# Splitting one weight piece over two DMA queues, and reading the residual from rows that are already loaded

## The chip, the cores and the metric

The kernel runs on 1 core of one Trainium2 chip. The metric is the device time of one execution in microseconds (us). Before the change its median is 773.24 us over 3 runs (773.04 to 773.42).

## What is computed

One decode step for a batch of B = 2 tokens with model width D = 1024. A layer norm of x feeds two branches, and both are added to x itself, the residual:

```python
xn = _layernorm(x)                                  # x is (2, 1, 1024), no scale or shift
q  = (xn @ wq).reshape(2, 1, 32, 128)               # 32 query heads, 4 key and value heads
p  = softmax(q @ k_cache^T * 128 ** -0.5)           # k_cache, v_cache: (2, 4, 32768, 128)
A  = (p @ v_cache).reshape(2, 1, 4096) @ wo
Bo = silu(xn @ w1) @ w2                             # w1: 1024 x 3584, w2: 3584 x 1024
return x + A + Bo
```

All of it is float32. With two tokens the work is reading: the two caches (268 MB) and the weights pass through the core once.

## The kernel before

**Two buffers and one queue.** `bufA` and `bufB` hold 128 partitions x 16384 floats (8 MB each). SyncE (SP) issues all large loads on its own DMA queue, q1 in the profile, alternately into the two buffers, in a fixed order: `wq[0]`, `wq[1]`, `w1b`, `w1a`, then for each of the 8 pairs of a head and a token two loads of keys and two of values, then `wo[0]`, `wo[1]`, `w2a` (two halves) and last `w2b`. Before each load SP waits (`freed`) until TensorE is through with what the buffer held; `load()` (L161 to L164) does this. A load is spread over 16 DMA engines, and each of these works through its share of q1 in order.

**The end of the stream.** `w2b` is the last load, 12 x 1024 floats in each of 128 rows. It comes in seven pieces, cut by `cuts`: 6 D, 2 D, D, D, D, then 4 * CUT = 768 floats and the last 256 floats of each row. Each has its own semaphore (`ld[1]`, `more[1]`, `last[0]` to `last[4]`), so TensorE can begin on a piece when it lands. The five pieces of `last` are used by `tile(0)` to `tile(4)`, each 8 float32 matmuls into the PSUM tile `acc`. Their order on TensorE is written out by hand at the end of the function: tile 0, tile 1, then two products that fold the sum of everything else (`ob`) into `acc`, then tiles 2, 3 and 4. ScalarE copies `acc` to `ot` (L242), and SP writes `ot` to memory (L330) and waits for it.

**The sum of everything else.** ScalarE copies the partial products of `wo` and `w2` from PSUM to `ev[0]`, `ev[1]`, `ev[2]` (L240), each as soon as TensorE has finished them. GpSimd (POOL) copies the lhs weights for the next load into `weights` (L317), adds `ev[1]` to `ev[0]` (L319), adds the residual `xres` (L321) and `ev[2]` (L323); VectorE adds the two halves (L325) and then the first part of `w2b` (L327), which gives `ob`.

**x at the start.** ScalarE's DMA queue (q10) brings x in two small transfers. `x8` (L115) is 8 rows of 1024 floats into every 16th partition of `xs`: the two tokens four times, each copy rotated by another quarter, because only the first 256 columns of `xs` are normalised and transposed; the four copies cover the four quarters in different partitions. `x` (L117) is 4 rows of 512 floats into every 16th of the first 64 partitions of `xres`, a slice of the zeroed tile `blank`, for the residual.

Of the kernel before, what the change touches and what calls it, by code (L numbers as in the profile page):

```python
# [8 lines left out]
B, HQ, HKV, SK, DH, D, F = 2, 32, 4, 32768, 128, 1024, 3584  # L9
P = 128  # L10
REP = HQ // HKV
W = 16384
NC = SK // W
KT = D // P
FT = F // P
QW = D // 4
CUT = 3 * QW // 4
LOOPS = HKV * B
STEPS = 4 + 4 * LOOPS + 4
# [29 lines left out]
        self.eng.sem_inc(token, -n)  # L49


def gqa_plus_mlp_kernel(nc, x, x8, kt, v0, v1, wq, wo, w1a, w1b, w2a, w2b, out):


    pe, dve, act, pool = (Stream(nc, e, n) for e, n in
                          ((nc.tensor, "pe"), (nc.vector, "dve"), (nc.scalar, "act"), (nc.gpsimd, "pool")))
    sp, T, V, A, G = nc.sync, nc.tensor, nc.vector, nc.scalar, nc.gpsimd
    sems = [pe.sem, dve.sem, act.sem, pool.sem]

    def sem(name):  # L60
        sems.append(nc.alloc_semaphore(name))
        return sems[-1]

    def sb(name, *shape):
        return nc.alloc_sbuf_tensor(name, shape, F32).ap()
# [3 lines left out]

    buf = [sb(n, P, W) for n in ("bufA", "bufB")]  # L70
    ld, more, tok = ([sem(f"{n}{k}") for k in "AB"] for n in ("ld", "more", "tok"))
    ldx, ldr, done, turn_sem, self_sem = (sem(n) for n in ("ldx", "ldr", "done", "marks", "self"))
    freed, subbed, normed, tq, pself = (sem(n) for n in ("freed", "subbed", "normed", "tq", "pself"))
    trm, tgd, tls, tob = (sem(n) for n in ("trm", "tgd", "tls", "tob"))
    last = [sem(f"last{i}") for i in range(5)]
# [3 lines left out]
    xs, xT = sb("xs", P, D), sb("xT", P, KT, 32)  # L79
    stats, mv, ln = sb("stats", P, 2, V.BN_STATS_DIM), sb("mv", P, 2), sb("ln", P, 6)  # L80
    ev = [sb(f"ev{i}", P, 1024) for i in range(4)]
# [2 lines left out]
    pre, sig, rsig = sb("pre", P, FT, 32), sb("sig", P, FT, B), sb("rsig", P, FT, B)  # L84
    onew = sb("onew", P, REP)
    ones = sb("ones", P, P)
    blank, used = sb("blank", P, P + 32 + 160 + 3 * REP + 1024 + 32 * (HQ + FT)), [0]

    def zeroed(*shape):
        n = shape[0] * (shape[1] if len(shape) > 1 else 1)  # L90
        lo = used[0]
        used[0] += n
        t = blank[:, lo:lo + n]
        return t.rearrange("p (a m) -> p a m", m=shape[1]) if len(shape) > 1 else t

    ident, sel, fold, rm, lsum, gd, ob, xres = (zeroed(n) for n in (P, 32, 160, REP, REP, REP, 512, 512))
    oT, hT = zeroed(HQ, 32), zeroed(FT, 32)
    rest, ot = sb("rest", P, 512), sb("ot", P, QW)
    gm, gmax, rl = sb("gm", REP, 1), sb("gmax", P, 1, REP), sb("rl", P, REP)
# [5 lines left out]
    def mm(o, lhsT, rhs, start=True, stop=True):  # L105
# [7 lines left out]
    z = pool.mark(G.memset(blank, 0.0))  # L113
    act.wait(z_x)
    A.dma_start(xs[::16, :], x8).then_inc(ldx, 16)  # L115
    act.wait(z)
    A.dma_start(xres[0:64:16, :], x).then_inc(ldr, 16)  # L117
    sp.wait_ge(ldx, 16)
    sp.dma_start(buf[1], wq[1]).then_inc(ld[1], 16)

# [1 line left out]
    t = pool.mark(G.affine_select(out=ident, in_=ident, compare_op=ALU.not_equal, fill=1.0, base=0,  # L122
                                  pattern=[[-1, P]], channel_multiplier=1))
    pool.wait(t)
    halves = fold[:, 32:].rearrange("p (a m) -> p a m", m=64)[:, :, :32]
    t = pool.mark(G.tensor_add(halves, *(ident[:, 64 * g:64 * g + 64].rearrange("p (a m) -> p a m", m=32)
                                         for g in range(2))))
# [6 lines left out]
    for i in range(2):  # L134
        t = dve.mark(V.bn_stats(stats[:, i, :], xs[:, i * 512:(i + 1) * 512]))
    dve.wait(t)
    t = dve.mark(V.bn_aggr(mv, stats))
    var, std, y0, t0, t1, rstd = (ln[:, i:i + 1] for i in range(6))
    dve.wait(t)
    t = dve.mark(V.tensor_scalar_add(var, mv[:, 1:2], EPS))  # L140
    act.wait(t)
    t = act.mark(A.activation(std, var, AF.Sqrt))
    for f in (lambda: V.reciprocal(y0, std), lambda: V.tensor_mul(t0, y0, y0), lambda: V.tensor_mul(t1, t0, var),
# [5 lines left out]
        t = dve.mark(f())  # L149
# [11 lines left out]
    def load(k, dst, src, s, n):  # L161
        if n:
            sp.wait_ge(freed, n)
        sp.dma_start(buf[k][:, dst] if isinstance(dst, slice) else dst, src).then_inc(s, 16)  # L164
# [10 lines left out]
    load(0, slice(0, W // 2), w2a[:, :W // 2], ld[0], STEPS - 3)  # L175
    load(0, slice(W // 2, W), w2a[:, W // 2:], more[0], 0)
    cuts = [0, 6 * D, 8 * D, 9 * D, 10 * D, 11 * D, 11 * D + 4 * CUT, 12 * D]
    for lo, hi, s in zip(cuts, cuts[1:], [ld[1], more[1], *last]):
        load(1, slice(lo, hi), w2b[:, lo:hi], s, STEPS - 2 if lo == 0 else 0)


    for n in range(4):
        act.wait((freed, n + 1))
        t = act.mark(A.copy(ev[n], ps[n % 2]))
# [4 lines left out]
        a, b = ev[n][:, :512], ev[n][:, 512:]  # L189
        if n < 2:  # L190
            i_sumq = pool.mark(G.tensor_add(sumq[:, 512 * n:512 * n + 512], a, b))  # L191
        elif n == 2:
            t = pool.mark(G.tensor_add(sumh[:96, 512:], a[:96, :384], b[:96, :384]))
            for j in range(3):
                pool.wait(t)
                t = pool.mark(G.tensor_add(sumh[96:, 512 + P * j:512 + P * (j + 1)], a[32 * j:32 * j + 32, 384:],
                                           b[32 * j:32 * j + 32, 384:]))
# [15 lines left out]
    t = dve.mark(V.transpose(pre.rearrange("p t m -> p (t m)"), sumh))  # L213

    act.wait(t)
    t = act.mark(A.activation(sig, pre[:, :, ::16], AF.Exp, scale=-1.0))
    for f in (lambda: V.tensor_scalar_add(sig, sig, 1.0), lambda: V.reciprocal(rsig, sig),
              lambda: V.tensor_mul(hT[:, :, ::16], pre[:, :, ::16], rsig)):
        dve.wait(t)
        t = dve.mark(f())  # L220
# [16 lines left out]
    outs = []  # L237
    for n in range(3):
        act.wait((freed, STEPS - 3 + n))
        outs.append(act.mark(A.copy(ev[n], ps[n % 2])))  # L240
    act.wait((pe, 2))
    i_ot = act.mark(A.copy(ot, acc))  # L242
# [74 lines left out]
        G.tensor_copy(wt[c][:, :2 * n].rearrange("p (t d) m -> p t d m", d=2),  # L317
                      hT[:, 16 * c:16 * c + n, None, :].to_broadcast([P, n, 2, 32])).then_inc(tok[c], 1)
    t = pool.mark(G.tensor_add(ev[0], ev[0], ev[1]))  # L319
    pool.wait(t, (ldr, 16))  # L320
    t = pool.mark(G.tensor_add(ev[0][:, :512], ev[0][:, :512], xres))  # L321
    pool.wait(t, outs[2])
    t = pool.mark(G.tensor_add(ev[0], ev[0], ev[2]))  # L323
    dve.wait(t)
    t = dve.mark(V.tensor_add(rest, ev[0][:, :512], ev[0][:, 512:]))  # L325
# [64 lines left out]
    def quarter(o, lhsT, w, start=False, stop=False):  # L390
        return [mm(o[32 * j:32 * j + 32, :], lhsT[j], w[j], start, stop) for j in range(4)][-1]

    def tile(t, o, lo, n, start=False, stop=False):
        T.wait_ge(last[t], 16)
        at = buf[1][:, lo:lo + 4 * n].rearrange("p (j n) -> p j n", j=4)
        return quarter(o, [hT[:, min(24 + t, FT - 1), :]] * 4, [at[:, j] for j in range(4)], start, stop)

    pe.mark(tile(0, acc, 8 * D, QW, True))
    tile(1, acc, 9 * D, QW)
    T.wait_ge(tob, 1)  # L400
    for c in range(2):
        mm(acc, fold[:, 32 - 32 * c:160 - 32 * c], ob[:, c * QW:(c + 1) * QW], False, False)
    tile(2, acc, 10 * D, QW)
    tile(3, acc[:, :CUT], 11 * D, CUT)
    pe.mark(tile(4, acc[:, CUT:], 11 * D + 4 * CUT, QW - CUT, False, True))
# [46 lines left out]
```

## Time and profile before

| what | value |
|---|---|
| median of 3 runs | 773.24 us (773.04 to 773.42) |
| the profiled execution: its own time | 773.19 us |
| its span, first to last instruction | 771.8 us |
| around the span | 1.39 us |
| TensorE busy | 396.3 us (51%) |
| VectorE, GpSimd, ScalarE busy | 132.4, 45.4, 28.4 us |
| bytes moved by DMA | 331.43 MB, mean 429 GB/s |

The profile is of one execution, so sums are made against 773.19 us. Engines: PE is TensorE, PEld its weight loads, DVE VectorE, ACT ScalarE, POOL GpSimd, SP SyncE; a q behind the name (SPq, ACTq) is the engine's sequencer, which issues DMAs. L106 is the helper that issues every matmul, L44 the helper that passes a semaphore on, so those lines stand for many places. In a table by windows the columns are the window, its length, the busy time of each engine with the number of instructions, the granted TensorE clock, the mean busy share of the 16 DMA engines and GB/s. Packets are counted where they start, so the share in a short window can be over 1.

### The profile page before, as it was taken

Reading aid. Unit: us, or ns where it says so; the run is one execution under the profiler, and the core shown is the slowest. Engines: PE = TensorE matmul, PEld = TensorE weight load, DVE = VectorE, ACT = ScalarE, POOL = GpSimd, SP = SyncE. Lnnn points to the kernel's source line nnn. Section 1 sums busy time; section 2 is a strip of 40 time slices with the busy share of each in tenths; the row PEclk is TensorE's granted clock in tenths of the full one; section 3 lists DMA queues with packets and bytes.
Section 4 is the critical chain, followed back from the end, with each engine's and each line's share of the span. In section 5 each row is a group of like instructions: output and inputs, shape, how many; then the busy total and the mean of one; then the engine's idle time right before and its main releaser. Section 6 shows DMA issues by size and latency. Waiting matters only on the chain. (4 is left out here: it accounts for less than half of the span.)

```text
span 771.8 us, 6114 instructions
## 1 busy us (share of the span) xinstructions
PE 396.3 (51%) x2702; PEld 126.3 (16%) x2702; DVE 132.4 (17%) x99; ACT 28.4 (4%) x37; POOL 45.4 (6%) x73
## 2 busy tenths in 40 slices
PE   0545545464546454545454546554545454545566
PEld 0111111121112111211121112111211121112122
DVE  2000103030403030303130403031303130303000
ACT  0000100100010001000100010001000100010000
POOL 3001200001000100010001000100010001000121
PEclk9976766767776667776767776667776777776688
DMA  9999999999999999999999999999999999999997
GB/s 383 435 435 435 435 435 435 435 435 435 435 435 435 435 435 435 435 431 435 435 435 435 435 435 435 435 435 435 428 435 435 431 435 421 425 431 425 431 433 329
DMA packets 6953, 331.43 MB, mean 429 GB/s; under 512 B 780, under 2 KB 924, under 8 KB 1448
## 3 DMA queue, kind: packets, MB, share of 16 engines
q1 hardware_dynamic: 6928, 331.37, 99.4%
q10 hardware_dynamic: 24, 0.04, 0.0%
q8 instruction: 1, 0.02, 0.0%
HBM read 331.39 MB, written 0.02 MB: 429 GB/s over the span
## 5 line engine op out<-in xcount | busy, mean ns | idle before, releaser
L106 PE MATMUL xy<-bufB,weights 128*32 128x512 f32 x1248 | 179.6, 740 | 167.4 <-PEq L49 167.4
L106 PE MATMUL xy<-bufA,weights 128*32 128x512 f32 x1280 | 183.7, 738 | 96.9 <-PEq L49 96.9
L106 PEld LDWEIGHTS xy<-bufB,weights 128*32 128x32 f32 x1248 | 49.4, 133 | 297.8 <-issue 297.7
L106 PEld LDWEIGHTS xy<-bufA,weights 128*32 128x32 f32 x1280 | 50.6, 132 | 213.5 <-issue 213.4
L257 DVE STREAM_TRANSPOSE st<-xy 128x2048 f32<-128x2048 f32 x8 | 18.5, 2317 | 243.2 <-PE xy L106 243.2
L270 DVE TENSOR_REDUCE blank<-xy 128x512 f32<-128x2048 f32 x8 | 18.3, 2292 | 224.5 <-PE xy L106 224.5
L285 POOL MEMSET weights<- 128x1024 f32 x16 | 15.2, 951 | 525.4 <-POOLq L49 525.4
L106 PE MATMUL smA<-blank 128*8 128x128 f32 x20 | 5.4, 371 | 51.9 <-PEq L49 51.9
L106 PE MATMUL smA<-blank,ones 128*128 128x8 f32 x18 | 4.9, 347 | 50.6 <-PEq L49 50.6
L259 DVE TENSOR_REDUCE blank<-st 128x8 f32<-128x2048 f32 x8 | 30.5, 3808 | 0.3
L271 DVE TENSOR_REDUCE blank<-weights 128x8 f32<-128x2048 f32 x8 | 30.4, 3799 | 0.0
L233 ACT ACTIVATE weights<-st 128x1024 f32<-128x1024 f32 x16 | 16.0, 1048 | 328.3 <-DVE st L267 328.3
L267 DVE TENSOR_TENSOR st<-st,gmax 128x2048 f32<-128x2048 f32 x8 | 18.3, 2291 | 0.3
L106 PE MATMUL smB<-blank 128*128 128x8 f32 x72 | 15.9, 350 | 0.0
L106 PEld LDWEIGHTS smB<-blank 128*128 128x128 f32 x72 | 15.6, 318 | 0.0
L106 PEld LDWEIGHTS smA<-blank,ones 128*128 128x128 f32 x18 | 4.3, 298 | 58.5 <-issue 58.5
L236 ACT COPY blank<-onew 128x8 f32<-128x8 f32 x8 | 1.6, 204 | 279.5 <-DVE onew L275 279.5
L106 PEld LDWEIGHTS smA<-blank 128*8 128x8 f32 x20 | 1.3, 88 | 60.2 <-issue 60.2
L325 DVE TENSOR_TENSOR rest<-ev 128x512 f32<-128x512 f32 x1 | 0.7, 691 | 49.2 <-POOL ev L323 49.2
L290 POOL COPY weights<-qall 128x128 f32 x32 | 8.4, 291 | 4.2 <-POOL weights L285 3.1
L106 PE MATMUL smB<-blank,ones 8*128 8x8 f32 x20 | 5.3, 334 | 5.7 <-PEq L49 5.7
L209 DVE STREAM_TRANSPOSE tqs<-sumq 128x1024 f32<-128x1024 f32 x1 | 1.2, 1246 | 39.2 <-POOL sumq L191 39.2
(53 smaller groups left out, 58.2 us busy)
## 6 DMA issues: line engine op xcount, KB each, us to landing
bufA<-in_w2a SPq DMA_DIRECT2D x2, 4096.0 KB, 22.5
bufA<-in_w1b SPq DMA_DIRECT2D x1, 6144.0 KB, 23.7
bufB<-in_w2b SPq DMA_DIRECT2D x1, 3072.0 KB, 17.1
bufB<-in_w2b SPq DMA_DIRECT2D x3, 512.0 KB, 20.8
bufB<-in_w2b SPq DMA_DIRECT2D x1, 1024.0 KB, 19.2
bufB<-in_w2b SPq DMA_DIRECT2D x1, 384.0 KB, 22.1
bufA<-in_kt SPq DMA_DIRECT2D x8, 27.4
bufB<-in_kt SPq DMA_DIRECT2D x8, 29.0
```

Of the source, the lines that this page charges most:

```text
L106: return T.matmul(o, lhsT, rhs, start=start, stop=stop)
L209: i_q = dve.mark(V.transpose(tqs.rearrange("p c m -> p (c m)"), sumq))
L233: A.activation(wt[c].rearrange("p e m -> p (e m)"), st[:, 1024 * c:1024 * c + 1024], AF.Exp, scale=SCALE).then_inc(tok[c], 1)
L236: A.copy(oT[:, REP * h:REP * (h + 1), 16 * b], onew).then_inc(tq, 1)
L257: t = mine(V.transpose(st, xy))
L259: V.tensor_reduce(rm, e8.rearrange("p n m -> p m n"), AX.X, ALU.max).then_inc(trm, 1)
L267: V.tensor_sub(e8, e8, gmax.to_broadcast([P, 256, REP])).then_inc(subbed, 1)
L270: V.tensor_reduce(ob, xy.rearrange("p (c n) -> p n c", c=4), AX.X, ALU.add).then_inc(tob, 1)
L271: V.tensor_reduce(lsum, weights.rearrange("p e (r m) -> p m (e r)", m=REP), AX.X, ALU.add).then_inc(tls, 1)
L285: G.memset(wt[c], 0.0).then_inc(pself, 1)
L290: m = G.tensor_copy(o, q[:, None, None, :].to_broadcast([P, 4, 4, REP]))
L325: t = dve.mark(V.tensor_add(rest, ev[0][:, :512], ev[0][:, 512:]))
```

## The change

The piece of `w2b` that `tile(3)` uses (768 floats of each row) is no longer one transfer of 128 rows on SP's queue. SP brings its rows 0 to 63. ScalarE's queue brings rows 64 to 113 (50 rows) and rows 114 to 127 (14 rows), issued between the second wait for `freed` and the second of the three copies at L240; this is the wait that SP's first `w2b` load has too. `tile(3)` waits for three transfers (48) in place of one (16).

The transfer of `x`, its semaphore `ldr`, the slice `xres` and the two waits that belong to them are gone. The residual is added from `xs[:64, 256:768]`, which holds x as it was loaded. For this the copies in `x8` have their quarters in another order, and on the host the rows of `wq` and `w1` are put in the order that goes with it. `blank`, which is zeroed at the start, has 512 columns fewer.

```diff
-def gqa_plus_mlp_kernel(nc, x, x8, kt, v0, v1, wq, wo, w1a, w1b, w2a, w2b, out):
+def gqa_plus_mlp_kernel(nc, x8, kt, v0, v1, wq, wo, w1a, w1b, w2a, w2b, out):
...
-    blank, used = sb("blank", P, P + 32 + 160 + 3 * REP + 1024 + 32 * (HQ + FT)), [0]
+    blank, used = sb("blank", P, P + 32 + 160 + 3 * REP + 512 + 32 * (HQ + FT)), [0]
...
     A.dma_start(xs[::16, :], x8).then_inc(ldx, 16)
-    act.wait(z)
-    A.dma_start(xres[0:64:16, :], x).then_inc(ldr, 16)
...
-    for lo, hi, s in zip(cuts, cuts[1:], [ld[1], more[1], *last]):
-        load(1, slice(lo, hi), w2b[:, lo:hi], s, STEPS - 2 if lo == 0 else 0)
+    def part(i, rows):
+        return (buf[1][rows, cuts[i]:cuts[i + 1]], w2b[rows, cuts[i]:cuts[i + 1]])
+
+    for i, s in enumerate([ld[1], more[1], *last]):
+        load(1, *part(i, slice(0, 64 if i == 5 else P)), s, 0 if i else STEPS - 2)
...
         act.wait((freed, STEPS - 3 + n))
+        if n == 1:
+            for lo, hi in ((64, 114), (114, P)):
+                A.dma_start(*part(5, slice(lo, hi))).then_inc(last[3], 16)
         outs.append(act.mark(A.copy(ev[n], ps[n % 2])))
...
-    pool.wait(t, (ldr, 16))
-    t = pool.mark(G.tensor_add(ev[0][:, :512], ev[0][:, :512], xres))
+    pool.wait(t)
+    t = pool.mark(G.tensor_add(ev[0][:64, :512], ev[0][:64, :512], xs[:64, 256:768]))
...
-        T.wait_ge(last[t], 16)
+        T.wait_ge(last[t], 48 if t == 3 else 16)
...
-    w1 = np.asarray(B_w1)
+    wq, w1 = (np.asarray(a).reshape(4, QW, -1)[[2, 0, 1, 3]].reshape(D, -1) for a in (A_wq, B_w1))
...
-        "x": np.ascontiguousarray(xr.reshape(B, 2, 512).transpose(1, 0, 2)).reshape(4, 512),
-        "x8": np.stack([np.roll(xr, -QW * g, axis=1) for g in range(4)]).reshape(8, D),
+        "x8": np.stack([xr.reshape(B, 4, QW)[:, o] for o in ((2, 0, 1, 3), (0, 2, 3, 1), (1, 0, 2, 3), (3, 0, 1, 2))]
+                       ).reshape(8, D),
```

More of the change, by code (lines that the diff above doesn't have):

```diff
@@ L71, in gqa_plus_mlp_kernel @@
     ld, more, tok = ([sem(f"{n}{k}") for k in "AB"] for n in ("ld", "more", "tok"))
-    ldx, ldr, done, turn_sem, self_sem = (sem(n) for n in ("ldx", "ldr", "done", "marks", "self"))
+    ldx, done, turn_sem, self_sem = (sem(n) for n in ("ldx", "done", "marks", "self"))
     freed, subbed, normed, tq, pself = (sem(n) for n in ("freed", "subbed", "normed", "tq", "pself"))
@@ L94, in zeroed @@
         return t.rearrange("p (a m) -> p a m", m=shape[1]) if len(shape) > 1 else t
-    ident, sel, fold, rm, lsum, gd, ob, xres = (zeroed(n) for n in (P, 32, 160, REP, REP, REP, 512, 512))
+    ident, sel, fold, rm, lsum, gd, ob = (zeroed(n) for n in (P, 32, 160, REP, REP, REP, 512))
     oT, hT = zeroed(HQ, 32), zeroed(FT, 32)
@@ L434 @@
         "v1": lay(v[:, :, 1], (B, HKV, 2, 4, 4, 4, 4, 32, DH), (0, 1, 4, 7, 2, 5, 6, 3, 8), (B, HKV, P, W)),
-        "wq": np.stack([lay(A_wq, qd, (4, 0, 3, 1, 6, 2, 5, 7), (2, P, W))[0],
-                        lay(A_wq, qd, (4, 0, 3, 1, 2, 6, 5, 7), (2, P, W))[1]]),
+        "wq": np.stack([lay(wq, qd, (4, 0, 3, 1, 6, 2, 5, 7), (2, P, W))[0],
+                        lay(wq, qd, (4, 0, 3, 1, 2, 6, 5, 7), (2, P, W))[1]]),
         "wo": np.stack([lay(A_wo, split, (0, 4, 1, 3, 5, 2, 6), (2, P, W))[0],
```

## The prediction

> **What bounds the kernel now.** The page comes first, for the load on the DMA queues, together with the table by windows for the middle of the run and the waits of SP's queue.
>
> ```profile
> span 771.8 us, 6114 instructions
> ...
> q1 hardware_dynamic: 6928, 331.37, 99.4%
> q10 hardware_dynamic: 24, 0.04, 0.0%
> q8 instruction: 1, 0.02, 0.0%
> ```
>
> ```profile
> 40.00:740.00 700.00, 364.53 (x2458) 116.68 (x2462) 127.01 (x85) 23.46 (x31) 31.03 (x57) 0.73 1.00 433
> ```
>
> ```profile
> SPq L164 <- DVEq L44: 719.8, 38, 22.7
> ```
>
> SP's queue, q1, fills the 16 DMA engines for 99.4% of their span. From 40 to 740 us they are busy all the time (share 1.00) at 433 GB/s, that is 433 / 16 = 27.1 GB/s for one engine, while TensorE has 364.53 of 700 us. SP waits 719.8 us for a buffer and still the engines do not run dry, because the load before is then in flight. So time is bytes over 433 GB/s, plus a start and a tail, and only the bytes and the tail can be changed by this edit. The tail is next: the chain of waits, then the timeline of the last microseconds.
>
> ```profile
> 745.78 20.84 DMA bufB<-in_w2b
> 766.62 0.04 issue
> 766.66 2.91 PE acc L106 x36
> 769.57 0.02 issue
> 769.59 0.37 ACT ot L242
> ```
>
> ```profile
> 761.85 3.64 PE L106 MATMUL xy<-bufB,weights 128*32 128x512 f32 x32 [1.07 <-PEq L49]
> ...
> 766.16 0.69 DVE L327 TENSOR_TENSOR blank<-rest,xy 128x512 f32<-128x512 f32 x1 [1.00 <-PE acc L106]
> 766.66 0.64 PE L106 MATMUL acc<-bufB,blank 128*32 128x256 f32 x8 [0.64 <-DMA bufB<-in_w2b]
> 767.23 1.13 PE L106 MATMUL acc<-blank 128*128 128x256 f32 x4
> 768.29 1.23 PE L106 MATMUL acc<-bufB,blank 128*32 128x256 f32 x24
> 768.88 0.48 PEld L106 LDWEIGHTS acc<-bufB,blank 128*32 128x32 f32 x16 [0.43 <-DMA bufB<-in_w2b]
> ```
>
> The chain goes back from the output to a landing at 766.62. That is not the last piece: 36 matmuls follow it, 8 of tile 1, 4 of the fold and 24 of tiles 2, 3 and 4, so it is the landing of tile 1's piece. From there TensorE runs nearly without a gap to 769.57. The weight loads at 768.88 are the one place where it still waits for data: tile 3, the piece that the change splits. Tile 2 begins at 768.29, and 8 matmuls of that size took 767.23 - 766.66 = 0.57 us of TensorE's time at tile 1, so tile 3 could have begun at about 768.86 or a little earlier, and began at 768.88. The split piece thus holds the end by some hundredths of a microsecond, at most 0.1; the landing of tile 1 sets the rest.
>
> The windows show how the queue runs out.
>
> ```profile
> 764.00:766.00 2.00, 2.00 (x24) 0.47 (x16) 0.69 (x1) 0.00 (x0) 0.43 (x1) 1.00 1.01 403
> 768.00:768.15 0.15, 0.15 (x2) 0.00 (x0) 0.00 (x0) 0.00 (x0) 0.00 (x0) 1.00 0.16 55
> 768.15:768.36 0.21, 0.21 (x5) 0.07 (x8) 0.00 (x0) 0.00 (x0) 0.00 (x0) 1.00 0.04 15
> 768.36:768.72 0.36, 0.36 (x9) 0.09 (x8) 0.00 (x0) 0.00 (x0) 0.00 (x0) 1.00 0.07 23
> 768.72:769.20 0.48, 0.48 (x12) 0.17 (x11) 0.00 (x0) 0.00 (x0) 0.00 (x0) 1.00 0.00 0
> ```
>
> From 768.15 to 768.72 the share is 0.04 to 0.07, and one engine of 16 is 0.0625. So one engine works alone for the last 768.72 - 768.15 = 0.57 us. I take it that it is late by that much at every piece, tile 1's too. The q8 row names a candidate for the cause: one packet of 0.02 MB, about 0.6 to 0.7 us of one engine at 27.1 GB/s.
>
> **The split piece.** These are the transfers, from the list of DMA issues.
>
> ```profile
> bufB<-in_w2b SPq DMA_DIRECT2D x1, 384.0 KB, 22.1
> ...
> blank<-in_x ACTq DMA_DIRECT2D x1, 8.0 KB
> ```
>
> A row of the piece is 384 KB / 128 = 3 KB. At 403 GB/s, the rate at the tail, one engine moves 25.2 GB/s, so a row costs it 3072 / 25.2 = 0.122 us. Half the piece, 192 KB, is 0.49 us of all 16 engines.
>
> The change keeps the bytes. It takes 0.49 us of work from q1 at its end and puts the same work on q10 from about 745 us on, where ScalarE's wait for `freed` ends:
>
> ```profile
> 744.47 1.01 ACT L240 COPY ev<-xy 128x1024 f32<-128x1024 f32 x1 [16.70 <-DVEq L44]
> ...
> 745.54 0.61 POOL L317 COPY weights<-blank 128x512 f32<-128x512 f32 x1 [16.60 <-ACT ev L240]
> ...
> 748.57 1.26 POOL L321 TENSOR_TENSOR ev<-ev,blank 128x512 f32<-128x512 f32 x1
> 762.06 2.38 POOL L323 TENSOR_TENSOR ev<-ev 128x1024 f32<-128x1024 f32 x1 [12.23 <-ACT ev L240]
> ```
>
> The engines are full at that time, so whatever q10 moves early pushes q1 back. Everything between, tile 1's piece included, lands later; only tiles 3 and 4 get it back. If the 64 rows weigh equally on all engines, the landing of tile 1 goes from 766.62 to 767.11 and the 2.91 us of TensorE follow it. Tile 3 and tile 4 land as before, and so the hundredths up to 0.1 that tile 3 cost are gained back. The end moves by 0.49 less 0.02 to 0.1: about +0.43.
>
> No row shows which engines 50 or 14 rows go to, so the bounds come from the late engine. If it gets none of the 64 rows, tile 1's data on it stays at 766.62, and the others are 0.57 us ahead. Should ten of these get six rows each, they lose 6 x 0.122 = 0.73 and land at 766.62 - 0.57 + 0.73 = 766.78, so +0.16 at most and -0.1 at best. If the late engine is one that gets six rows, it is +0.73. The even split lies between, and I take that value, because nothing here tells which engine is late.
>
> [...]
>
> **ScalarE's two issues.** They stand ahead of the second copy at L240, and behind that copy wait POOL's L317, L319 and L321, then TensorE's last load of 128x512 products.
>
> ```profile
> 1.72 1.15 ACTq L115 DMA_DIRECT2D xs<-in_x  x1
> 4.49 0.53 ACTq L117 DMA_DIRECT2D blank<-in_x  x1
> ```
>
> Two issues cost 2 x 0.53 to 2 x 1.15, so 1.1 to 2.3 us. POOL's L317 would end at 746.15 + 2.3 = 748.5 at the latest, and TensorE needs it at 761.85. L321 would end at 749.83 + 2.3 = 752.1, and POOL's next step, L323, starts at 762.06 after ScalarE's third copy. So it costs nothing, with 10 to 13 us of cover. Without the cover the whole 1.1 to 2.3 us would show.
>
> **x at the start, and the residual.** The transfer that is gone is 8 KB: 8192 / 433 = 0.02 us of all engines. Its issue took 0.53 us of ScalarE while the first weights were loading.
>
> ```profile
> 1.62 2.84 POOL L113 MEMSET blank<- 128x3288 f32 x1
> ...
> 10.78 1.29 DVE L135 BATCH_NORM_STATS2 stats<-xs 128x6 f32<-128x512 f32 x2 [10.78 <-DMA xs<-in_x]
> ```
>
> The memset of `blank` loses 512 of 3288 columns, 0.44 us of POOL; but VectorE starts the norm at 10.78, when `xs` has landed, long after POOL is done, so this is hidden. The order of quarters changes no instruction. L321 works on 64 partitions in place of 128, with the same 512 columns: I keep its 1.26 us, and in either direction it has the cover above. `ldr` ended long before L321, so its wait goes for nothing. Together -0.02 us.
>
> Sum: 773.19 + 0.43 - 0.02 = 773.6 us for an execution like the profiled one. The median of the runs, 773.24, is 0.05 above it, which I do not add; it is within their spread.
>
> **The rivals.** *The late engine is spared.* Then tiles 3 and 4 come early and tile 1 on time: -0.1 at best, about 773.1. For it speaks the engine alone at the end; against it, that tile 1 and not the last piece sets the end, so the 0.57 us cannot be cashed in. Chance 0.22.
>
> *Both halves collide inside.* Rows 0 to 63 alone are written by all engines, and rows 64 to 127 beside q1's. If partitions in one half are written at half speed, each 192 KB costs 0.98 in place of 0.49 us: tile 1 is late by 0.98 and tile 3 by 0.49, so the end is about +0.9: 774.1. Nothing before writes only half of the partitions with such a load, so the profile speaks neither way. [...] Chance 0.25.
>
> *Few engines carry the 50 rows: slower.* The place is q10's first transfer. With it on 2 engines, each has 25 rows, 25 x 0.122 = 3.05 us, and tile 1 waits for them: 773.19 + 3.05 - 0.1 = 776.1. It decides from (1.55 + 0.1) / 0.122 = 14 rows on the late engine, or 1.65 + 0.57 = 2.22 us, 18 rows, on another. In the first 20 us the q10 transfers of 8 and 4 rows left 12 small packets,
>
> ```profile
> DMA packets 150, 8.25 MB, mean 412 GB/s; under 512 B 12, under 2 KB 12, under 8 KB 24
> ```
>
> as many completion words as rows, which fits one engine to a row; that speaks for a wide spread, at least for small counts. A late engine with six rows and the collision together (0.73 + 0.98) would come to the same side, near 774.8. Chance of this side 0.13.
>
> *The change does not do what it says:* q10 might be served only when q1 runs dry. Then the 64 rows come last, at the old time or with another issue's latency: 773.2. Alternate service at the start speaks against it (x lands at 10.78 with 8 MB of q1 still under way). Chance 0.03, counted in the middle.
>
> **How the numbers follow.** The even or partly uneven shift (773.2 to 773.9, likeliest 773.6) has 0.34, sparing 0.22, the collision 0.25, slower 0.13, unserved 0.03, and 0.03 is left for a gain over 0.2% that I cannot build from these rows: the tail has 0.6 us to give. 0.2% is 1.55 us, about what a measurement of this kernel can tell from no change. So faster 0.03, within 0.2% 0.84, slower 0.13. The range goes from 773.0 (sparing, with the runs' 0.2 us of spread) to 774.7 (the collision with an uneven share), and leaves the few engines out.
>
> **What the changed profile would show.** Right: q1 has 0.2 MB less and q10 0.2 MB more; the chain still ends in tile 1's landing, at 767.0 to 767.2, with some 2.9 us of TensorE behind it, and the weight loads of tile 3 no longer wait. Sparing: the share at the end stays over 0.0625 until the queue is empty, and tile 1 lands at 766.6 to 766.8. Collision: tile 3's wait grows, and the rate in the windows at 745 to 755 or at the end falls. Wrong altogether: a chain that ends in ScalarE, in POOL's L321, or in a wait for tile 3 of more than 1 us.

## The result and the profile after

The changed kernel takes 775.67 us (median of 8 runs, 775.23 to 776.06) against 773.24 us (773.04 to 773.42): 2.43 us slower, ratio 1.0031, 95% interval 1.002 to 1.0042. That is above the range, and past the 0.2% that the prediction drew as its line. Its profiled execution took 775.32 us, with a span of 774.0 us, against 773.19 and 771.8 before. Ratios and intervals go by fast runs alone: one of the ten executions of the run with every second row, below, took 993.87 us, was slow, and is not in its ratio.

The page of the changed kernel, its totals and DMA queues:

```profile
span 774.0 us, 6114 instructions
...
DMA packets 6969, 331.42 MB, mean 428 GB/s; under 512 B 800, under 2 KB 944, under 8 KB 1464
...
q1 hardware_dynamic: 6864, 331.17, 99.3%
q10 hardware_dynamic: 104, 0.23, 0.1%
```

The bytes are as planned: 0.2 MB went from q1 to q10. q10 had 104 packets. 16 of them fall in the first 20 us, the 8 rows of x and 8 packets under 512 B; the 64 rows of the piece are 64, and 24 are left. These are small too: on the whole page the packets under 512 B went from 780 to 800, 24 more for the piece and 4 fewer for the transfer of `x`. (With 48 and 16 rows, in a run below, q10 had 112 packets, so 32 small ones for the piece.) If each engine that a transfer uses leaves one small packet, which no view shows, then with 16 engines neither transfer used fewer than 24 - 16 = 8, and ten for the 50 rows and fourteen for the 14 would fit. So the rows did not go over a few, as far as a count of packets can say.

The chain of waits of the changed kernel, its end (start, length, what):

```profile
747.03 23.32 DMA bufB<-in_w2b
770.35 0.04 issue
770.39 0.64 PE acc L106 x8
771.03 0.01 issue
771.05 0.69 PE acc L106 x16
771.73 0.02 issue
771.76 0.37 ACT ot L247
```

The landing that sets the end is now that of tile 2's piece, at 770.35, with 24 matmuls behind it; before it was tile 1's. The timeline of the same stretch:

```profile
768.34 0.64 PE L106 MATMUL acc<-bufB,blank 128*32 128x256 f32 x8 [0.65 <-DMA bufB<-in_w2b]
768.90 0.73 PEld L106 LDWEIGHTS acc<-blank 128*128 128x128 f32 x4 [0.41 <-DVE blank L332]
768.90 1.13 PE L106 MATMUL acc<-blank 128*128 128x256 f32 x4
770.39 0.16 PEld L106 LDWEIGHTS acc<-bufB,blank 128*32 128x32 f32 x8 [0.76 <-DMA bufB<-in_w2b]
770.39 1.30 PE L106 MATMUL acc<-bufB,blank 128*32 128x256 f32 x24 [0.36 <-DMA bufB<-in_w2b]
```

Tile 1 starts at 768.34, which is 1.68 later than the 766.66 of before. Tile 2 starts at 770.39, 2.10 later than 768.29, and TensorE sat idle for it for 0.36 us. So most of the loss is made before tile 1 lands, and a second, smaller part between tile 1 and tile 2. The table by windows of the changed kernel shows both places:

```profile
744.00:749.00 5.00, 5.00 (x48) 1.54 (x40) 0.00 (x0) 1.01 (x1) 1.93 (x2) 1.00 1.01 428
749.00:757.00 8.00, 1.42 (x12) 0.45 (x12) 0.00 (x0) 0.00 (x0) 2.26 (x2) 0.85 1.02 359
757.00:766.00 9.00, 7.65 (x52) 2.09 (x48) 0.13 (x1) 1.01 (x1) 2.38 (x1) 0.75 0.96 402
766.00:768.30 2.30, 1.69 (x20) 0.31 (x12) 1.03 (x2) 0.00 (x0) 0.00 (x0) 1.00 1.03 411
768.30:769.30 1.00, 0.96 (x10) 0.53 (x11) 0.22 (x1) 0.00 (x0) 0.00 (x0) 1.00 1.05 233
```

The same windows of the kernel before, the last one shifted to the same distance behind tile 1's landing:

```profile
749.00:757.00 8.00, 2.61 (x16) 0.78 (x20) 0.00 (x0) 0.00 (x0) 0.83 (x1) 0.76 1.02 439
```

```profile
766.60:767.60 1.00, 0.94 (x10) 0.50 (x11) 0.25 (x1) 0.00 (x0) 0.00 (x0) 1.00 1.00 387
```

From 749 to 757 us, while q10 brings rows 64 to 127, the engines are as busy as before (1.02) but move 359 GB/s in place of 439: 8 x (439 - 359) / 433 = 1.5 us lost. Behind tile 1, while rows 0 to 63 come, they move 233 in place of 387 at full share. Busy engines with a lower rate mean that packets take longer. Whose packets, the rows of the two queues say. These are packets, MB and the share of 16 engines' time from 744 to 758 us, the changed kernel first:

```profile
q1 hardware_dynamic: 192, 5.21, 96.9%
q10 hardware_dynamic: 87, 0.20, 4.0%
```

and the kernel before:

```profile
q1 hardware_dynamic: 225, 6.04, 100.3%
```

q10's packets took 4.0% of 16 engines for 14 us, which is 0.14 us for each of its 64 rows, small packets counted in; that is near the forecast's estimate of 0.122. It is q1 that slowed. Its packets moved 5.21 MB in 0.969 x 14 = 13.57 us, so 384 GB/s, where those of before moved 430. At 430 GB/s the 5.21 MB would have taken 1.45 us less.

### The profile page after: what moved, and what is told of

Read it like the earlier page. It is cut to its first block, busy times and chain, and to the rows that moved or that the text cites. A ratio compares the mean times of both kernels' runs of the same rounds, so it can differ in the third digit from the quotient of the medians.

```text
span 774.0 us, 6114 instructions
## 1 busy us (share of the span) xinstructions
PE 397.4 (51%) x2702; PEld 126.7 (16%) x2702; DVE 132.4 (17%) x99; ACT 28.3 (4%) x37; POOL 44.9 (6%) x73
## 5 line engine op out<-in xcount | busy, mean ns | idle before, releaser
L106 PE MATMUL xy<-bufB,weights 128*32 128x512 f32 x1248 | 182.1, 748 | 168.6 <-PEq L49 168.6
```

What stands on the lines that cost most here:

```text
L106: return T.matmul(o, lhsT, rhs, start=start, stop=stop)
```

## Experiments

Theory A: a transfer of 64 neighbouring rows writes one half of the partitions, and this is slow, early and late. Theory B: a second queue beside the first costs by itself. Theory C: the uneven counts of rows cost, 50 and 14, neither a multiple of 16. (A row of the piece goes to the partition of its number, so rows 0 to 63 are one half of the partitions and rows 64 to 127 the other.) All edits are against the changed kernel; each ratio is against the runs of the kernel before on the same chip. Three chips were used: one for the first four runs; one for every second row, halves early, 48 and 16 and the whole piece; one for halves late, the uneven spread and the other half. Three dots mark where a cut leaves lines out. The line with the count for which `tile(3)` waits is shown for the first run only; in the others it follows the number of transfers.

**The x part alone** (`e1_x_only`)

```diff
-        load(1, *part(i, slice(0, 64 if i == 5 else P)), s, 0 if i else STEPS - 2)
+        load(1, *part(i, slice(0, P)), s, 0 if i else STEPS - 2)
...
-        if n == 1:
-            for lo, hi in ((64, 114), (114, P)):
-                A.dma_start(*part(5, slice(lo, hi))).then_inc(last[3], 16)
...
-        T.wait_ge(last[t], 48 if t == 3 else 16)
+        T.wait_ge(last[t], 16)
```

> The change without the split: the piece comes whole by SyncE, x's own transfer stays away. Theory A (transfers that reach one half of the partitions slow all engines): no such transfer is left, so 773.2, within 0.2 of before. Theory B (packets of a second queue among the first's slow all engines, whichever partitions they write): the same, 773.2, since ScalarE's queue is empty after the start. If the loss came from the x part, this run is at 775 or more.

Measured: 773.15 us against 773.15, ratio 0.9999 (0.999 to 1.0009). The x part neither costs nor brings anything that shows; the whole loss is the split.

**All three groups on SyncE** (`e2_all_on_sp`)

```diff
-        load(1, *part(i, slice(0, 64 if i == 5 else P)), s, 0 if i else STEPS - 2)
+        for lo, hi in ((0, 64), (64, 114), (114, P)) if i == 5 else ((0, P),):
+            load(1, *part(i, slice(lo, hi)), s, 0 if i else STEPS - 2)
...
-        if n == 1:
-            for lo, hi in ((64, 114), (114, P)):
-                A.dma_start(*part(5, slice(lo, hi))).then_inc(last[3], 16)
```

> The same three groups of rows (64, 50 and 14), all issued by SyncE in the piece's old place, nothing on ScalarE's queue. Theory A: both halves of the piece are at half rate at the end of the stream, 2 x 0.49 us more, so about 774.2, with a rate near 230 GB/s while they run and no loss from 749 to 757 us. Theory B: no second queue, so no loss but the ten rows in place of eight on the late engine, 0.24 us: 773.4 to 773.5.

Measured: 773.9 us against 773.15, ratio 1.0009 (1.0 to 1.0019). It lies between the two expectations; that the late engine has ten rows in place of eight was an assumption, and no view shows it. The windows of this run show the slow end without any second queue:

```profile
749.00:757.00 8.00, 2.69 (x16) 0.83 (x20) 0.00 (x0) 0.00 (x0) 0.30 (x1) 0.70 1.00 431
...
767.00:768.00 1.00, 1.00 (x12) 0.68 (x4) 0.00 (x0) 0.00 (x0) 0.00 (x0) 1.00 0.97 212
```

212 GB/s at a share of 0.97, so theory B is not needed for the end. Tile 1 starts at 766.61 in this trace, as before (766.66), but tile 2 at 769.08, with TensorE idle for 0.77 us. So the three groups of rows delay tile 2's piece, although they stand behind it in the queue.

**Split by columns** (`e3_columns`)

```diff
+    def cols(lo, hi):
+        return (buf[1][:, cuts[5] + lo:cuts[5] + hi], w2b[:, cuts[5] + lo:cuts[5] + hi])
...
-        load(1, *part(i, slice(0, 64 if i == 5 else P)), s, 0 if i else STEPS - 2)
+        src = cols(0, 2 * CUT) if i == 5 else part(i, slice(0, P))
+        load(1, *src, s, 0 if i else STEPS - 2)
...
-            for lo, hi in ((64, 114), (114, P)):
-                A.dma_start(*part(5, slice(lo, hi))).then_inc(last[3], 16)
+            A.dma_start(*cols(2 * CUT, 4 * CUT)).then_inc(last[3], 16)
```

> The piece is split by columns: SyncE brings 384 of 768 floats for all 128 rows, ScalarE the other 384, also for all 128 rows, at the same time as in the change. The same 192 KB goes by the second queue, but every transfer reaches all partitions, and each engine carries the same. Theory A: only the bytes move, 0.49 us earlier on the queue and 0.49 later for tile 1, so 773.6 to 773.8, with the rate from 749 to 757 us at 410 or more. Theory B: the loss from 749 to 757 us stays at 1.4 us or more (twice the packets at half the size could make it larger), so 774.7 to 776, without the half rate at the end.

Measured: 773.55 us against 773.15, ratio 1.0005 (0.9996 to 1.0015). Windows of this run:

```profile
749.00:757.00 8.00, 2.48 (x12) 0.69 (x16) 0.00 (x0) 0.00 (x0) 1.39 (x2) 0.80 1.01 426
```

The same bytes by the same second queue at the same time cost 0.40 us and not 2.43. Theory B falls: when every transfer reaches all partitions, mixing the queues costs no more than the 0.49 us of the moved bytes, as far as the interval can tell.

**One transfer of 64 rows** (`e4_one_of_64`)

```diff
-            for lo, hi in ((64, 114), (114, P)):
-                A.dma_start(*part(5, slice(lo, hi))).then_inc(last[3], 16)
+            A.dma_start(*part(5, slice(64, P))).then_inc(last[3], 16)
```

> ScalarE brings rows 64 to 127 as one transfer in place of 50 and 14. If the uneven rows (six on the late engine) are what costs, it gets four and the time falls by 2 x 0.12 us, to 775.4, or more if the others wait for it. Theory A: the same one half of the partitions, so as slow as the change, 775.2 to 775.9, rate from 749 to 757 us near 360, half rate at the end. Theory B: as slow too, since the second queue moves the same bytes.

Measured: 774.9 us against 773.15, ratio 1.0021 (1.0011 to 1.0031). Windows of this run:

```profile
749.00:757.00 8.00, 1.35 (x15) 0.31 (x12) 0.00 (x0) 0.00 (x0) 2.30 (x2) 0.66 1.03 392
```

64 rows, a multiple of 16, and still 1.75 us slower, with a slow stretch from 749 to 757 (392 GB/s). So theory C is not the main cause. The time is below every expectation, though: theory A had 775.2 to 775.9, as slow as the change, and a rate near 360. But the change is 0.7 us slower still, more than the 2 x 0.12 us that two rows more would cost one engine by the estimate of 0.122 us for a row.

**Every second row** (`e5_every_second`)

```diff
-        load(1, *part(i, slice(0, 64 if i == 5 else P)), s, 0 if i else STEPS - 2)
+        load(1, *part(i, slice(0, P, 2 if i == 5 else 1)), s, 0 if i else STEPS - 2)
...
-            for lo, hi in ((64, 114), (114, P)):
-                A.dma_start(*part(5, slice(lo, hi))).then_inc(last[3], 16)
+            A.dma_start(*part(5, slice(1, P, 2))).then_inc(last[3], 16)
```

> SyncE brings rows 0, 2, 4 and so on, ScalarE rows 1, 3, 5 and so on: 64 rows each, but every transfer reaches all parts of the 128 partitions. Theory A1 (the cost is that 64 neighbouring partitions are one half of the ways into the memory): no loss beside the moved bytes, 773.5 to 773.7, rate from 749 to 757 us at 415 or more, no half rate at the end. Theory A2 (the cost is that an engine writes partitions other than those it writes in a transfer of 128 rows): as slow as the one transfer of rows 64 to 127, 774.7 to 775.2, with the rate near 390.

Measured: 773.47 us against 773.2, ratio 1.0003 (0.9993 to 1.0013). Windows of this run:

```profile
749.00:757.00 8.00, 1.92 (x12) 0.68 (x16) 0.00 (x0) 0.00 (x0) 0.58 (x1) 0.66 1.03 438
```

It differs from the run before by which 64 rows go together, nothing else: 438 GB/s in place of 392, and 1.75 - 0.27 = 1.5 us less. So the choice of rows makes the loss, and not their number or their bytes. A1 forecast this time; but A2 falls only if the alternate rows go to other engines than in a transfer of 128 rows, and no view shows which engine writes which row. Between the two this run does not decide.

**Halves only early, and halves only late** (`e6_halves_early`, `e11_halves_late`). ScalarE brings 384 columns and SyncE the other 384; in the first run ScalarE's part is cut into rows 0 to 63 and 64 to 127, in the second SyncE's.

```diff
-        load(1, *part(i, slice(0, 64 if i == 5 else P)), s, 0 if i else STEPS - 2)
+        src = cols(0, 2 * CUT) if i == 5 else part(i, slice(0, P))
+        load(1, *src, s, 0 if i else STEPS - 2)
...
-            for lo, hi in ((64, 114), (114, P)):
-                A.dma_start(*part(5, slice(lo, hi))).then_inc(last[3], 16)
+            for lo, hi in ((0, 64), (64, P)):
+                A.dma_start(*cols(2 * CUT, 4 * CUT, slice(lo, hi))).then_inc(last[3], 16)
```

```diff
-        load(1, *part(i, slice(0, 64 if i == 5 else P)), s, 0 if i else STEPS - 2)
+        for src in [cols(0, 2 * CUT, slice(lo, lo + 64)) for lo in (0, 64)] if i == 5 else [part(i, slice(0, P))]:
+            load(1, *src, s, 0 if i else STEPS - 2)
...
-            for lo, hi in ((64, 114), (114, P)):
-                A.dma_start(*part(5, slice(lo, hi))).then_inc(last[3], 16)
+            A.dma_start(*cols(2 * CUT, 4 * CUT)).then_inc(last[3], 16)
```

`cols` is the helper of the run split by columns, with the rows as a third argument.

> ScalarE brings columns 384 to 767 as two transfers, rows 0 to 63 and rows 64 to 127; SyncE brings columns 0 to 383 of all rows. The 192 KB of ScalarE's queue are the same in bytes as in the run split by columns, and only cut into halves of the partitions; nothing at the end of the stream is cut. Theory A: the loss from 749 to 757 us is there (rate 380 to 400), the end runs at its old rate, so the time lies between: 774.0 to 774.5. If the early half cost nothing and all the loss were at the end, it is 773.6.

> ScalarE brings columns 384 to 767 of all 128 rows early, as in the run split by columns (773.55); SyncE brings columns 0 to 383 at the piece's old place as two transfers, rows 0 to 63 and rows 64 to 127. Only the end of the stream is cut into halves. Theory A: 192 KB at half rate at the end, up to 0.49 us more, and less where the second half fills the ways that the first leaves free: 773.7 to 774.1, with no loss from 749 to 757 us. If halves cost only beside a second queue: 773.55.

Measured, early: 774.32 us against 773.2, ratio 1.0014 (1.0005 to 1.0024); late: 773.59 us against 773.21, ratio 1.0008 (0.9998 to 1.0018). Windows of the early one:

```profile
749.00:757.00 8.00, 1.50 (x8) 0.46 (x12) 0.00 (x0) 0.00 (x0) 1.35 (x2) 0.69 1.01 393
```

and of the late one:

```profile
749.00:757.00 8.00, 2.38 (x12) 0.68 (x16) 0.00 (x0) 0.00 (x0) 0.22 (x1) 0.64 1.03 439
...
767.00:768.00 1.00, 0.96 (x10) 0.52 (x11) 0.24 (x1) 0.00 (x0) 0.00 (x0) 1.00 1.06 256
```

192 KB cut into halves early cost 1.12 - 0.40 = 0.72 us over the same bytes uncut. The two intervals overlap, but the windows say the same: 393 GB/s in place of 426 is 8 x 33 / 433 = 0.6 us. (The early run also has one transfer more than the uncut one.) Cut late, the halves cost nothing that can be told from the uncut 773.55, though the rate dips there too, and in the trace TensorE waits 0.20 us for tile 2. Each late half is 96 KB, half of what the change sends that way.

**48 and 16 rows** (`e7_48_and_16`)

```diff
-            for lo, hi in ((64, 114), (114, P)):
+            for lo, hi in ((64, 112), (112, P)):
```

> The change with 48 and 16 rows in place of 50 and 14: still two transfers on ScalarE's queue, but each spreads evenly over 16 engines, three rows and one. If the 0.77 us between the change and the run with one transfer of 64 rows come from the uneven rows (six on ten engines, the late one among them), this run is at 774.9, within 0.2. If they come from the second transfer, it is at 775.5 to 775.8.

Measured: 775.29 us against 773.2, ratio 1.0026 (1.0016 to 1.0036). Windows of this run:

```profile
749.00:757.00 8.00, 0.73 (x4) 0.23 (x8) 0.00 (x0) 0.00 (x0) 0.83 (x1) 0.65 0.97 367
```

Neither expectation: it is 2.09 over its before, half way between one transfer (1.75) and 50 and 14 (2.43). A second transfer of neighbouring rows and the uneven spread seem to cost some 0.3 us each; the intervals, about 0.001 of 773 or 0.8 us to either side, do not separate them. The rates of q1 at the end of this section point the same way, with one trace for each.

**The whole piece early** (`e8_whole_early`)

```diff
-        load(1, *part(i, slice(0, 64 if i == 5 else P)), s, 0 if i else STEPS - 2)
+        if i != 5:
+            load(1, *part(i, slice(0, P)), s, 0 if i else STEPS - 2)
...
-            for lo, hi in ((64, 114), (114, P)):
-                A.dma_start(*part(5, slice(lo, hi))).then_inc(last[3], 16)
+            A.dma_start(*part(5, slice(0, P))).then_inc(last[3], 16)
```

> ScalarE brings the whole piece, 128 rows of 768 floats, in one transfer at the time of the change; SyncE brings none of it. Twice the bytes by the second queue, all partitions. Theory A (only bytes count where all partitions are reached): tile 1 is 0.98 us later in place of 0.49, so 774.0 to 774.2, with a rate near 430 from 749 to 757 us. Theory B (the second queue costs by itself): more than that, 775 or above.

Measured: 774.03 us against 773.2, ratio 1.0011 (1.0002 to 1.0021). Twice the bytes, twice the cost in the median (0.83 after 0.40), as theory A has it: where every transfer reaches all partitions, the moved bytes account for the cost.

**Uneven, but spread over the partitions** (`e9_uneven_spread`)

```diff
-        load(1, *part(i, slice(0, 64 if i == 5 else P)), s, 0 if i else STEPS - 2)
+        load(1, *part(i, slice(0, P, 2 if i == 5 else 1)), s, 0 if i else STEPS - 2)
...
-            for lo, hi in ((64, 114), (114, P)):
-                A.dma_start(*part(5, slice(lo, hi))).then_inc(last[3], 16)
+            for lo, hi in ((1, 101), (101, P)):
+                A.dma_start(*part(5, slice(lo, hi, 2))).then_inc(last[3], 16)
```

> Every second row as in that run, but ScalarE's 64 rows as 50 and 14, so ten engines carry five rows more and fourteen one more. If uneven rows cost what their bytes are, the late engine has six in place of four, 2 x 0.12 us, and a second transfer adds little: 773.6 to 774.0 against 773.47. If unevenness and the second transfer cost 0.4 us each by themselves, as they did on neighbouring rows, it is 774.2 to 774.4.

Measured: 774.5 us against 773.21, ratio 1.0016 (1.0006 to 1.0026). Windows of this run:

```profile
749.00:757.00 8.00, 1.72 (x10) 0.49 (x14) 0.00 (x0) 0.00 (x0) 2.35 (x2) 0.75 1.04 400
```

1.0 us more than the even spread, and a slow stretch again (400 against 438 GB/s). Two rows more on the late engine, 0.24 us by the same estimate, would explain a quarter of it. q10 had 104 packets here as in the change, so again 24 small ones, which fits ten and fourteen engines. The time is nearest to the second expectation, in which unevenness and a second transfer cost by themselves. No half is cut here: the 50 rows are the odd ones from 1 to 99, the 14 those from 101 to 127. So neighbouring rows are not needed for a slow stretch, and A1 is not the whole rule. Fewer engines at once, or engines that write other rows than in a whole piece (A2), remain as explanations.

**The other half** (`e10_other_half`)

```diff
-        load(1, *part(i, slice(0, 64 if i == 5 else P)), s, 0 if i else STEPS - 2)
+        load(1, *part(i, slice(64 if i == 5 else 0, P)), s, 0 if i else STEPS - 2)
...
-            for lo, hi in ((64, 114), (114, P)):
-                A.dma_start(*part(5, slice(lo, hi))).then_inc(last[3], 16)
+            A.dma_start(*part(5, slice(0, 64))).then_inc(last[3], 16)
```

> The halves change places: ScalarE brings rows 0 to 63 early in one transfer, SyncE rows 64 to 127 at the end. Theory A1 (any 64 neighbouring rows are half of the ways): as slow as with rows 64 to 127 early, 774.9 within 0.3. If only the upper half is narrow, or the late engine matters by where it writes, it differs by 0.5 or more.

Measured: 774.85 us against 773.21, ratio 1.0022 (1.0012 to 1.0031), so the same as with the upper half early. It does not matter which half it is.

**q1 alone, in every run.** The rows of the queues from 744 to 758 us give the rate of q1's own packets, its bytes over the time they took. Unlike the rates in the windows it does not depend on where a window cuts a packet.

| runs | what the second queue brings early | q1's rate, GB/s |
|---|---|---|
| before, the x part alone, all on SyncE | nothing | 430 |
| by columns, halves late, whole piece | transfers of all 128 rows | 429 to 430 |
| every second row | one transfer of 64 rows | 430 |
| one of 64, the other half, halves early | 64 neighbouring rows at a time | 403 to 404 |
| uneven, but spread | 50 and 14 rows, alternate | 404 |
| 48 and 16 | neighbouring rows | 393 |
| the change, 50 and 14 | neighbouring rows | 384 |

At 430 GB/s the bytes of q1 would have taken 0.8 to 0.9 us less at 403 to 404, 1.17 us less at 393 and 1.45 us less at 384; in the other runs the loss is below 0.05 us. On neighbouring rows, the second transfer (404 or 403 to 393) and the uneven spread (393 to 384) thus add some 0.3 us each to the early loss. The halves early come as two transfers and stay at 404, so a second transfer does not always add.

## Why the prediction was wrong

**What bounds the kernel: right, but in another place.** It is the engines' time at the tail; the chain still ends in a landing of `w2b`, but in tile 2's and not in tile 1's, with 1.4 us of TensorE behind it (770.39 to 771.76) and not 2.9. Of the signs that the prediction named for a collision, the rate did fall, early and late, while the idle time in front of tile 3's weight loads hardly grew (0.43 to 0.49 us).

**Moving bytes forward costs tile 1: right, and 0.43 us well sized.** With columns and with every second row it measured 0.40 and 0.27 us in the median, and 0.83 for twice the bytes, each within some 0.8 us to either side. In the traces tile 1's piece lands at 766.94, 767.15 and 767.35 in these three runs, against 766.57 with the x part alone.

**The x part and ScalarE's issues: right.** -0.02 was forecast, too little to be seen, and nothing was seen. The issues were cheaper than the bounds of 1.1 to 2.3 us, and hidden:

```profile
745.23 0.73 ACTq L244 DMA_DIRECT2D bufB<-in_w2b  x2
...
750.08 1.25 POOL L326 TENSOR_TENSOR ev<-ev,xs 64x512 f32<-64x512 f32 x1
...
763.46 2.38 POOL L328 TENSOR_TENSOR ev<-ev 128x1024 f32<-128x1024 f32 x1 [12.12 <-ACT ev L245]
```

That is the timeline of the changed kernel: two issues in 0.73 us, and L326 ends 12 us before L328 can start.

**The step that failed: the 64 rows were charged their own bytes, and the stream beside them nothing.** In the sum, tile 1 is late by 0.49 us of bytes and the end by 0.43. The rows themselves cost about what was said, 0.14 us each. But q1's packets slowed beside them, from 430 to 384 GB/s, and this costs 1.45 us. With the moved bytes, 0.40 us, that is 1.85 us, near the 1.68 us by which tile 1 starts late.

**The rival "Both halves collide inside" had the collision and priced it too low.** It had a chance of 0.25 and +0.9 us; one transfer of 64 rows at a time, without any unevenness, measured +1.75. Of these 0.40 are the moved bytes, 0.72 the half early, and the other 0.63 (1.75 - 1.12) what the single half at the end adds; that last number is a difference of two runs, with the width of their intervals. No run shows that one half of the partitions is written at half speed; what the runs show in its place is 233 GB/s against 387 behind tile 1, a factor of 0.60, and q1 at 403 to 404 against 430 early. Two terms were too small. The early half was priced at its own bytes at half speed, 0.49 us over the moved bytes, and cost 0.72 by the times and 0.8 to 0.9 by q1's rate. The late half was taken to hide behind tile 1, since it was charged to tile 3 alone. It delays tile 2, whose piece is ahead of it in the queue: in the changed kernel tile 2 starts 2.10 late where tile 1 is 1.68 late, and with all rows on SyncE tile 2 is late while tile 1 is not.

**The uneven rows and the second transfer** add the remaining 0.7 us (2.43 - 1.75). The forecast had a late engine with six rows and the collision together, near 774.8, and so the right side; the mechanism was another, since by q1's rate these two also act through the stream beside them. That one engine is late at every piece, on which the ends of the range in part rested, no run here tests. Nor does any show an engine with six of the 64 rows, the term in the +0.16, the +0.73 and the upper end; what the runs show in its place is 2.43 us for 50 and 14 rows against 2.09 for 48 and 16, with q1 at 384 against 393 GB/s.

The bounds of the unknown cost were taken from what the 64 rows themselves would take, and nothing in them allowed the rest of the stream to be slowed.

Halves of the partitions as the cause agree with the trace at the end (233 in place of 387 GB/s), and with the every-second-row run, at 438 GB/s, in the middle. They do not account for the uneven run, whose 50 rows lie in both halves and which fell to 400 GB/s.

**The few engines: did not happen.** The 24 small packets fit ten and fourteen engines, if each engine leaves one, and tile 1 is 1.68 us late, not the 3.05 us that 25 rows on one engine would cost by the forecast's estimate. That the time fell on the side of that rival is luck; the mechanism was another.

**Open.** Why q1's packets slow, and at what grain (halves, or smaller groups of partitions, as the uneven run suggests), is not settled: the runs change which rows go together, and no view here shows a single way into the memory, or which engine writes which row. A1 and A2 are thus both open as reasons. The parts of the second transfer and of the uneven spread, 0.3 us each, come from one trace of each run, and the times do not separate them.

No version beats the kernel before: the x part alone equals it (0.9999), and every way of sending part of the piece early is slower in the median, since tile 1 needs its data before the piece does.

## What to carry to other kernels

Where a stream already fills the DMA engines, as here (share 1.00 from 40 to 740 us), do not expect a transfer issued earlier on a second queue to fill a gap: 192 KB as columns moved tile 1's landing from 766.57 to 766.94 us, and the whole piece, 384 KB, to 767.35. The question is which landing sets the end. If a piece must be divided, cut it by columns, or take every second row, so that each transfer is spread over the whole range of partitions; 64 neighbouring rows cost 1.5 us more here than 64 alternate ones. And keep such a part one transfer, of a multiple of 16 rows: alternate rows as 50 and 14 cost 1.0 us more than as 64. Whether the second transfer or the uneven count cost this, the runs do not separate. Last, bound an unknown transfer not only by its own duration but by what it can do to the transfers beside it.

## What the runs showed of the hardware

A transfer of 64 neighbouring rows on one queue, 192 KB or 0.06% of the bytes, lowered the rate of the packets of the other queue from 430 to 403 GB/s, as a mean over the 14 us from 744 to 758; as 48 and 16 rows it lowered it to 393, as 50 and 14 to 384, with the engines at a share of 0.97 to 1.04 from 749 to 757 us. Its own packets took 0.14 us for a row of 3 KB in the change, against the 0.122 estimated from the rate at the tail. The same 192 KB as 64 alternate rows, or as half the columns of all rows, left the rate at 429 to 430; 50 and 14 alternate rows did not (404). Transfers of 64, 50 and 14 neighbouring rows at the end of a queue delayed the piece that stands ahead of them in the same queue (TensorE idle for 0.77 us with all rows on SyncE). A second queue by itself cost nothing beyond its bytes that shows: 0.40 us for 192 KB and 0.83 us for 384 KB.
